# Attention head steps 8 to 11: probabilities and values as fp16 pairs, transposed by DMA, in place of fp32 on TensorE

## The chip, the cores and the metric

The kernel runs on one core of a Trainium2 chip. The metric is the device time of one execution in microseconds (us), as the median of several runs. Beside it there is one execution taken by the hardware profiler, from which all rows below come. TensorE is called PE here, VectorE DVE, ScalarE ACT, GpSimd POOL, and SP is the engine that only issues DMAs.

## The reference, cut to what matters

A decayed causal attention is followed by two feed-forward stages; only the attention and the first stage lie near the change.

```python
scores = q @ k.T / sqrt(D) + (cum[:, None] - cum[None, :])   # causal; cum = cumsum(log f)
attn = softmax(scores)                                       # B=4, H=8, S=576, D=64
x = (attn @ v) -> [B*S, H*D] = [2304, 512]
h = relu(x @ w_in); y = (h*h) @ w_out                        # d_ff = 2048
out = top-2 of 8 experts on y                                # 1024 wide each
```

## The kernel before, in words

**Attention is cut in two.** The first 256 positions of each batch (the head) are done early in twelve steps, numbered j = 0 to 11 (`subs`). Steps 8 to 11 are the second 128 queries of batches 2 and 3, four attention heads each. One head step is: fp32 scores S (`hd_s`, L397 to L408, on two PSUM banks of 512 columns), row maximum on DVE (`hd_max`, L419), exponentials on ACT (`hd_exp`, L430, result `pr`, fp32), eight fp32 transpositions of `pr` on PE (`hd_flip`, L436), their copy out of PSUM on ACT (`hd_copy`, L442, result `pth`), and eight fp32 products with V (`hd_pv`, L457), which the trace shows as sixteen records. After both steps of a batch the sum is normalized on DVE and ACT and turned into the columns of `xT` by a DMA (`att_turn`, L365). The positions from 256 on (the rest, units (b, i, p)) are done later; there P and V are already split into fp16 high and low parts (L277, L278, L208, L209), P is turned by a DMA (L279), and three fp16 products (L319) are made.

**The first feed-forward stage runs meanwhile.** It goes over chunks c of 384 tokens and over 16 weight tiles i: `mm1` (L554, twelve matmuls, one PSUM bank `m1`), relu and squares on ACT (L561, L562, L565), the low part g on DVE (L570), `mm2` (L616, nine matmuls). Passes: chunk 0 with weights 0 to 7 (in the hand-written order `PLAN`), chunk 1 with weights 0 to 7, then chunk 0 and chunk 1 with weights 8 to 15. Weights arrive packed and are unpacked by five operations each: three on DVE (L519, L524, L528), one on ACT (L531), and a last one on DVE (L534). They are staged in two buffers, so that the load of weight i+2, issued by POOL (L510), waits for the L534 of weight i. I write conv i for the five operations of weight i.

**What sets the order.** Up to the end of `PLAN` each engine's order is written out by hand; behind it a list scheduler with a cost model of its own places the instructions of all engines, once, ahead of the run. Each engine then goes through its row in order. `hd_tick(j)` at steps 8 to 13 of the feed-forward issues the head steps: the flip of step j-1, the scores of j, the PV of j-2.

**What is queued behind the weights.** POOL issues the last weight load (weight 15), then fills rows of the query sets (L178 to L180, 8.4 us), then issues the small DMAs `setk<-c` (L201), which bring the decay sums into the key sets. The scores of the rest (L226) wait for these. SP issues loads, spills and DMA transpositions in one row.

Of the kernel before, what the change touches and what calls it, by code (L numbers as in the profile page):

```python
# [7 lines left out]
F32 = mybir.dt.float32  # L8
F16 = mybir.dt.float16
# [31 lines left out]
NB = 2  # L41
# [18 lines left out]
R4 ch2 XT2 C31 ca3 E40 P3 cl2 h2 cb3 T40 lw4 E41 s3 l2 C40 T41 n3 cc3 S5 C41 ch3 XT3 R5 P4 h3 ca4 E50  # L60
m0 l3 cb4 E51 T50 cl3 r0 T51 cc4 lw5 X12 v21 C50 m1 g0 C51 ch4 S6 r1 cl4 g1 P5 R6 lw6 X13 v31 m2 s5 E60 ca5 a0 n5
r2 cb5 T60 h5 cc5 E61 m3 g2 ca6 ch5 l5 T61 r3 cb6 O5 a1 cl5 C60 C61 S7 g3 lw7 cc6 P6 R7 ch6 a2 cl6
E70 E71 m4 ca7 cb7 T70 r4 cc7 T71 C70 g4 a3 ch7 C71 cl7 m5 P7 r5 a4 s7 g5 n7 m6 h7 l7 O7 a5 r6
g6 m7 r7 g7
"""

# [2 lines left out]
def attn_moe_moe_kernel(ctx: ExitStack, tc, qka, qk, v, f, w_io, wgn, noise, w1, w2, out):  # L69
# [410 lines left out]
    def hd_xlow(j):  # L480
        b, i, a = subs[j]
        t0 = 128 * (B * i + b)
        nc.vector.tensor_tensor(xT[:, 1, :, t0:t0 + 128], hd["xf", j], xT[:, 0, :, t0:t0 + 128], op=ALU.subtract)  # L483

    def hd_tick(j, bank):
        if NPL <= j - 1 < NSUB:
            for z in range(2):
                hd_flip(j - 1, z, bank)
                hd_copy(j - 1, z)
        if j < NSUB:  # L490
            hd_s(j, bank)
            hd_max(j)
            for z in range(2):
                hd_exp(j, z)
        if NPL <= j - 2 < NSUB:
            hd_pv(j - 2)
            b, i, a = subs[j - 2]
            if a == i:
                att_sum(sums[b, i], 2, 2.0 ** -8, 1.6e-8)
                xs = att_norm(po_t[b, i], sums[b, i], 2)  # L500
                xh = att_high(xs, 2)
                att_low(xh, xs, 2)
                att_turn(b, i, xh)
# [482 lines left out]
    for tok in PLAN.split():  # L986
# [16 lines left out]
        elif tok[0] == "X" and tok[1] != "T":  # L1003
            hd_load(*d)
        elif tok[0] == "v":
            hd_load_v(*d)
        elif tok.startswith("lw"):
            pin["sp"] = load_w(d[0]).ins
        elif tok.startswith("c"):
            {"ca": conv_shift, "cb": conv_top, "cc": conv_rest, "ch": conv_high, "cl": conv_low}[tok[:2]](d[0])  # L1010
        elif tok[0] == "S":
            hd_s(d[0], start_bank if d[0] < NPX else main_bank)
        elif tok[0] == "R":
            hd_max(d[0])
        elif tok[0] == "E":
            hd_exp(*d)
        elif tok[0] == "T":
            hd_flip(d[0], d[1], flip_bank if d[0] < NPX else main_bank)
        elif tok[0] == "C":
            hd_copy(*d)  # L1020
        elif tok[0] == "P":
            hd_pv(d[0])
        elif tok[0] == "s":
            hd_sum(d[0])
        elif tok[0] == "n":
            hd_norm(d[0])
        elif tok.startswith("XT"):
            hd_xflip(d[0], xflip_bank)
        elif tok[0] == "h":
            if d[0] < NPX:  # L1030
                hd_xhigh(d[0])
            else:
                hd["xh", d[0]] = att_high(hd["n", d[0]], 2)
        elif tok[0] == "l":
            if d[0] < NPX:
                hd_xlow(d[0])
            else:
                att_low(hd["xh", d[0]], hd["n", d[0]], 2)
        elif tok[0] == "O":
            att_turn(subs[d[0]][0], subs[d[0]][1], hd["xh", d[0]])  # L1040
        elif tok[0] == "m":
            if psM is None:
                start_st.close()
                psM = mid_st.enter_context(tc.tile_pool(name="psM", bufs=1, space=PSUM))
            mm1_pe(0, d[0])
        elif tok[0] == "r":
            pin["act"] = mm1_act(0, d[0])
        elif tok[0] == "g":
            pin["dve"] = mm1_low(0, d[0])
        elif tok[0] == "a":  # L1050
            mm2(0, d[0])
        else:
            raise ValueError(tok)
# [223 lines left out]
```

## Time and profile before

| | |
|---|---|
| median of 3 runs | 985.39 us (984.55 to 988.39) |
| profiled execution: its own time | 986.78 us |
| its span, first to last instruction | 985.1 us |
| PE busy | 948.0 us (96%) |
| DVE busy | 563.3 us (57%) |
| ACT busy | 444.6 us (45%) |
| mean granted PE clock, 1 being full | 0.989 |

Busy time is the sum of an engine's instructions, overlaps counted once. Matmuls are pipelined, so a group's cost on PE is read from start to start and not from the duration of one. The head steps of the change lie between 88 and 141 us of the span.

### The profile page before, as it was taken

What the parts mean: (1) busy time and instruction counts of PE and PEld (TensorE: products, weight loads), DVE (VectorE), ACT (ScalarE), POOL (GpSimd) and SP (SyncE); (2) the same over time, 40 slices, a digit from 0 to 9 for tenths busy, and PEclk for the clock granted to TensorE, in tenths of its full rate; (3) what the DMA queues carried; (4) which work ended last, traced back from release to release, by engine and by line L of the source; (5) the groups of instructions that cost most, each with busy time, mean ns of one, the idle gap of its engine ahead of it and who ended that gap; (6) DMA issues with size and microseconds to landing.
All of it is one profiled execution on the core that took longest, in us unless ns stands there. A gap on an engine that the chain in (4) does not pass through costs nothing.

```text
span 985.1 us, 17576 instructions
## 1 busy us (share of the span) xinstructions
PE 948.0 (96%) x6866; PEld 552.9 (56%) x6866; DVE 563.3 (57%) x1240; ACT 444.6 (45%) x986; POOL 201.8 (20%) x238
## 2 busy tenths in 40 slices
PE   5899998999999999999999799999999999999996
PEld 3766664555555555555555344647475656565662
DVE  5884879777798778776477232436253434334221
ACT  3765659776577657645464120424141323223110
POOL 3000114004031021003002405244232314111202
PEclk9999999999999999999999899999999999999998
DMA  7374537695979949637295733698959494941303
GB/s 285 129 255 155 169 108 249 161 253 139 231 161 252 222 99 227 144 60 103 51 328 179 147 89 53 120 227 192 234 133 206 97 232 91 231 85 31 42 12 42
DMA packets 211255, 153.26 MB, mean 156 GB/s; under 512 B 166994, under 2 KB 177698, under 8 KB 209122
## 3 DMA queue, kind: packets, MB, share of 16 engines
q1 hardware_dynamic: 198994, 122.71, 49.5%
q0 software_dynamic: 12032, 29.35, 14.1%
q8 instruction: 55, 0.90, 0.4%
q14 instruction: 30, 0.25, 0.1%
q10 hardware_dynamic: 144, 0.05, 0.0%
HBM read 88.97 MB, written 23.98 MB: 115 GB/s over the span
## 4 chain that ended last, share of the span: by engine, by line
PE 76%; DMA 10%; issue 5%; DVE 4%; POOL 3%; ACT 1%; SPq 1%; ACTq 0%; POOLq 0%; DVEq 0%
PE e L882 18%; PE e L899 17%; PE m L554 15%; PE acc L616 14%; PE po L319 2%; DMA xgT<-xg 2%; DMA out_dram<-y,tix 2%; DMA wr<-in_w_dram 2%; DMA setk<-c 1%; PE psab L397 1%; PE po L457 1%; PE po L322 1%; DMA w<-in_w_io_dram 1%; PE ps L226 1%; PE ps L225 1%
## 5 line engine op out<-in xcount | busy, mean ns | idle before, releaser
L882 PE MATMUL e<-xgT,w1s 128*128 128x310 f16 (+2 forms) x1536 | 207.7, 297 | 6.0 <-DMA xgT<-xg 6.0
L899 PE MATMUL e<-w2s,hT 128*128 128x512 f16 (+1 forms) x960 | 209.3, 379 | 0.1
L616 PE MATMUL acc<-w,g 128*128 128x512 f16 x864 | 205.2, 379 | 0.4 <-DVE g L570 0.4
L882 PEld LDWEIGHTS <-w1s 128*128 128x128 f16 x1536 | 140.2, 98 | 72.4 <-issue 10.1
L886 ACT ACTIVATE hT<-e 128x310 f16<-128x310 f32 (+2 forms) x128 | 54.8, 429 | 269.4 <-PE e L882 269.1
L554 PE MATMUL m<-xT,w 128*128 128x384 f16 x960 | 173.1, 330 | 1.8 <-DVE xT L483 1.2
L899 PEld LDWEIGHTS <-hT 128*128 128x128 f16 (+1 forms) x960 | 99.5, 104 | 106.6 <-DVE hT L887 0.5
L554 PEld LDWEIGHTS <-w 128*128 128x128 f16 x1152 | 109.6, 99 | 77.1 <-issue 7.3
L616 PEld LDWEIGHTS <-g 128*128 128x128 f16 x864 | 81.5, 98 | 86.7 <-DVE g L570 0.7
L902 DVE TENSOR_SCALAR y<-e,gs 128x512 f32<-128x512 f32 (+1 forms) x40 | 30.0, 751 | 156.8 <-PE e L899 131.5
L887 DVE SCALAR_TENSOR_TENSOR hT<-e,hT 128x310 f16<-128x310 f32 (+2 forms) x128 | 60.8, 478 | 83.3 <-ACT hT L886 82.8
L903 POOL DMA_INDIRECT out_dram<-y,tix x40 | 65.6, 1641 | 164.2 <-DVE y L902 121.3
L764 POOL DMA_INDIRECT table<-ent,si x36 | 41.0, 1139 | 166.3 <-DVE si L761 156.8
L561 ACT ACTIVATE r<-m 128x384 f32<-128x384 f32 x80 | 39.1, 489 | 67.5 <-PE m L554 67.3
L254 DVE TENSOR_REDUCE sm<-ps 128x1 f32<-128x384 f32 (+2 forms) x96 | 53.3, 564 | 20.6 <-PE ps L242 9.4
L840 POOL DMA_INDIRECT xg<-x2d,tix x40 | 45.6, 1141 | 83.8 <-DMA xgT<-xg 53.5
L257 ACT ACTIVATE pr<-ps,sm 128x384 f32<-128x384 f32 (+1 forms) x64 | 40.1, 630 | 25.7 <-DVE sm L256 25.7
L562 ACT ACTIVATE g<-r 128x384 f16<-128x384 f32 x96 | 50.0, 521 | 1.8
L571 DVE TENSOR_TENSOR r<-r 128x384 f32<-128x384 f32 x64 | 35.5, 554 | 25.3 <-ACT g L562 25.1
L805 DVE SCALAR_TENSOR_TENSOR w2s<-wr,w2s 128x1024 f16<-128x1024 f32 x32 | 39.2, 1226 | 18.4 <-ACT w2s L804 18.4
L278 DVE TENSOR_TENSOR phl<-pr,phl 128x384 f16<-128x384 f32 (+1 forms) x64 | 38.6, 621 | 14.2 <-ACT phl L277 13.7
L805 DVE SCALAR_TENSOR_TENSOR w1s<-wr,w1s 128x1024 f16<-128x1024 f32 x32 | 38.9, 1224 | 11.9 <-ACT w1s L804 11.8
(276 smaller groups left out, 1076.4 us busy)
## 6 DMA issues: line engine op xcount, KB each, us to landing
wr<-in_w_dram SPq DMA_DIRECT2D x64, 512.0 KB, 4.7
qkr<-in_qk_dram SPq DMA_DIRECT2D x16, 896.0 KB, 5.8
w<-in_w_io_dram SPq DMA_DIRECT2D x8, 1024.0 KB, 4.8
w<-in_w_io_dram POOLq DMA_DIRECT2D x8, 1024.0 KB, 6.2
vr<-in_v_dram SPq DMA_DIRECT2D x16, 320.0 KB, 3.7
x2d<-x SPq DMA_DIRECT2D x18, 256.0 KB, 2.6
hraw<-in_qka_dram SPq DMA_DIRECT2D x8, 512.0 KB, 5.9
out_dram<-zero SPq DMA_DIRECT2D x5, 768.0 KB, 6.7
```

The source lines that it names most:

```text
L254: seen[u] = nc.vector.tensor_reduce(sm[:, z:z + 1], ps[z][:, :N], AX.X, ALU.max).ins
L554: nc.tensor.matmul(ps, W[i][:, wi, 0, 128 * cc:128 * cc + 128], xT[:, xi, cc, r0:r0 + CH], start=(x == 0), stop=(x == 11))
L562: nc.scalar.activation(g[:, 0, :], r, AF.Square, scale=2.0 ** -10)
L616: last[0] = nc.tensor.matmul(acc[t], g[:, gi, 128 * t:128 * t + 128], W[i][:, wi, 1, :], start=(i in ends[c][0] and x == 0), stop=(i in en ...
L764: s_ = nc.gpsimd.indirect_dma_start(out=table, out_offset=bass.IndirectOffsetOnAxis(ap=si[:, t, k:k + 1], axis=0), in_=ent[:, t, k, :], in ...
L805: nc.vector.scalar_tensor_tensor(lo, t_, sc, hi, op0=ALU.mult, op1=ALU.subtract)
L840: nc.gpsimd.indirect_dma_start(out=xg, out_offset=None, in_=x2d[0:seen, :], in_offset=bass.IndirectOffsetOnAxis(ap=rows_t[key, j][0], axis=0))
L882: last[0] = nc.tensor.matmul(ps[:, :hw], w1s[:, cc, wi, 128 * i:128 * i + 128], xgT[:, 4 * xi + cc, c], start=(x == 0), stop=(x == 11)).ins
L886: relu[0] = nc.scalar.activation(hi, ps[:, :hw], AF.Relu).ins
L887: nc.vector.scalar_tensor_tensor(hT[:, i, 1, c], ps[:, :hw], 0.0, hi, op0=ALU.max, op1=ALU.subtract)
L899: last[0] = nc.tensor.matmul(ps[:m], hT[:, i, hi, 128 * j:128 * j + m], w2s[:, i, wi, :], start=(i == 0 and x == 0), stop=(i == NFE - 1 an ...
L903: s_ = nc.gpsimd.indirect_dma_start(out=out, out_offset=bass.IndirectOffsetOnAxis(ap=ix[:m], axis=0), in_=y[:m], in_offset=None, compute_o ...
```

## The change

Steps 8 to 11 take the way of the later units. Values are split ahead of time (`hd_values`, tokens y0 to y3 in `PLAN`: one ACT and one DVE operation over 128x1024 each). P is split by two ACT and two DVE operations of 128x512 (`hd_split`), turned by one DMA transposition of 16 blocks on SP, and multiplied in 24 fp16 products of 64 columns (`hd_pv16`). Eight transpositions and eight fp32 products on PE and two copies on ACT go away in each step. The scale and floor of the sum follow the scale of V.

```diff
-E70 E71 m4 ca7 cb7 T70 r4 cc7 T71 C70 g4 a3 ch7 C71 cl7 m5 P7 r5 a4 s7 g5 n7 m6 h7 l7 O7 a5 r6
+E70 E71 m4 ca7 cb7 T70 r4 cc7 T71 C70 g4 y0 y1 a3 ch7 C71 cl7 m5 P7 r5 a4 s7 g5 y2 y3 n7 m6 h7 l7 O7 a5 r6
...
+    def hd_values(j):
+        b, i, a = subs[j]
+        vs = astream.tile([128, NB, 4, 2, 64], F16, name="vh", tag="vs", bufs=4)
+        vr = HV[b][:, :, 256 * a:256 * a + 256].rearrange("p k (h d) -> p k h d", h=4)
+        nc.scalar.activation(vs[:, :, :, 0, :], vr, AF.Copy, scale=64.0)
+        nc.vector.scalar_tensor_tensor(vs[:, :, :, 1, :], vr, 64.0, vs[:, :, :, 0, :], op0=ALU.mult, op1=ALU.subtract)
+        hd["v", j] = vs
+
+    def hd_split(j):
+        pr = hd.pop(("e", j))
+        phl = astream.tile([128, 4, 2, 2, 128], F16, name="phl", bufs=3)
+        pt = astream.tile([128, 4, 2, 2, 128], F16, name="pt", bufs=3)
+        for h in range(2):
+            pv = pr[:, h, :].rearrange("p (k s) -> p k s", s=128)
+            nc.scalar.activation(phl[:, :, h, 0, :], pv, AF.Copy)
+            nc.vector.tensor_tensor(phl[:, :, h, 1, :], pv, phl[:, :, h, 0, :], op=ALU.subtract)
+        nc.sync.dma_start_transpose(out=pt.rearrange("p a b c q -> p (a b c) q"), in_=phl.rearrange("p a b c s -> p (a b c s)"))
+        hd["t", j] = pt
+
+    def hd_pv16(j):
...
+        for p in range(2):
+            for z in range(2):
+                for kb in range(NB):
+                    for x, (vi, pi_) in enumerate(HL3):
+                        nc.tensor.matmul(po[:, a, z, p, :], pt[:, 2 * p + kb, z, pi_, :], vs[:, kb, 2 * p + z, vi, :],
+                                         start=(kb == 0 and x == 0), stop=(kb == i and x == 2), skip_group_check=True)
...
     def hd_tick(j, bank):
         if NPL <= j - 1 < NSUB:
-            for z in range(2):
-                hd_flip(j - 1, z, bank)
-                hd_copy(j - 1, z)
+            hd_split(j - 1)
...
-            hd_pv(j - 2)
+            hd_pv16(j - 2)
...
-                att_sum(sums[b, i], 2, 2.0 ** -8, 1.6e-8)
+                att_sum(sums[b, i], 2, 0.25, 1.024e-6)
...
+        elif tok[0] == "y":
+            hd_values(NPL + d[0] % NPL)
```

The scheduler places everything behind `PLAN` anew. In the changed file the lines behind the new functions stand 30 lower (L519 becomes L549, L534 becomes L564). SP's row of DMAs in the chunk-1 pass reads before (L365 turns x, L596 spills the accumulators, L643 to L665 set up the router's tables):

```order
29 L365 DMA_TRANSPOSE xT<-xh 128x8x128
30 L596 DMA part<-sp 128x1024 x3
31 L643 DMA wgr<-in_wgn_dram 128x64
32 L659 DMA table<-ini 128x8x8
33 L659 DMA table<-ini 128x8x2
34 L665 DMA table<-ino 128x8x28
35 L365 DMA_TRANSPOSE xT<-xh 128x8x128 x2
36 L596 DMA part<-sp 128x1024 x3
```

and now (L501 is the new transposition, L695 the old L665):

```order
29 L365 DMA_TRANSPOSE xT<-xh 128x8x128
30 L501 DMA_TRANSPOSE pt<-phl 128x16x128
31 L626 DMA part<-sp 128x1024 x3
32 L501 DMA_TRANSPOSE pt<-phl 128x16x128
33 L673 DMA wgr<-in_wgn_dram 128x64
34 L689 DMA table<-ini 128x8x8
35 L689 DMA table<-ini 128x8x2
36 L695 DMA table<-ino 128x8x28
37 L501 DMA_TRANSPOSE pt<-phl 128x16x128
38 L365 DMA_TRANSPOSE xT<-xh 128x8x128
39 L501 DMA_TRANSPOSE pt<-phl 128x16x128
40 L365 DMA_TRANSPOSE xT<-xh 128x8x128
```

The third transposition (step 10) stands right behind the table DMA, and the fourth behind the turn of batch 2.

DVE's row late in the chunk-1 pass, before (w_1384 is weight 11, w_1440 weight 12, L570 a g):

```order
131 L524 SCALAR_TENSOR_TENSOR w_1384<-w_1148,w_1384 128x1024
132 L528 SCALAR_TENSOR_TENSOR w_1148<-w_1148,w_1384 128x1024
133 L346 TENSOR_TENSOR xh<-xs,xh 128x512
134 L570 TENSOR_TENSOR g<-r,g 128x384
135 L519 TENSOR_SCALAR w_1440<-w_1244 128x1024
136 L534 SCALAR_TENSOR_TENSOR w_1384<-w_1148,w_1384 128x1024
137 L524 SCALAR_TENSOR_TENSOR w_1440<-w_1244,w_1440 128x1024
```

and now (w_1420 is weight 11, w_1492 weight 12, L600 a g, L500 the new low part of P for step 11):

```order
142 L554 SCALAR_TENSOR_TENSOR w_1420<-w_1154,w_1420 128x1024
143 L600 TENSOR_TENSOR g<-r,g 128x384
144 L144 SCALAR_TENSOR_TENSOR c_85<-c_85,pm,fch 96x320
145 L331 TENSOR_SCALAR sums<-sums 128x8
146 L558 SCALAR_TENSOR_TENSOR w_1154<-w_1154,w_1420 128x1024
147 L500 TENSOR_TENSOR phl<-pr,phl 128x4x128
148 L332 RECIPROCAL sums<-sums 128x8
149 L500 TENSOR_TENSOR phl<-pr,phl 128x4x128
150 L600 TENSOR_TENSOR g<-r,g 128x384
151 L549 TENSOR_SCALAR w_1492<-w_1260 128x1024
152 L564 SCALAR_TENSOR_TENSOR w_1420<-w_1154,w_1420 128x1024
153 L554 SCALAR_TENSOR_TENSOR w_1492<-w_1260,w_1492 128x1024
```

The split of P stands inside the unpacking of weight 11, which ends two splits later in the row.

On PE the first product with weight 15 (mm1 of chunk 0), which has to wait for conv 15, stood behind mm2 of weights 12 to 14 for two of the three token blocks (w_1845 is weight 15, w_1540 weight 14):

```order
1308 L616 MATMUL acc_1660<-w_1540,g 128x512
1309 L616 LDWEIGHTS g
1310 L616 MATMUL acc_1660<-w_1540,g 128x512
1311 L554 LDWEIGHTS w_1845
1312 L554 MATMUL m_1996<-xT,w_1845 128x384
```

and now it stands directly behind the scores of the third unit, ahead of all mm2 of weights 12 to 14 (w_1897 is weight 15):

```order
1402 L226 LDWEIGHTS setq_1721
1403 L226 MATMUL ps<-setk_1720,setq_1721 128x384
1404 L227 LDWEIGHTS identw
1405 L227 MATMUL ps<-maskw,identw 128x128
1406 L584 LDWEIGHTS w_1897
1407 L584 MATMUL m_2048<-xT,w_1897 128x384
```

So mm2 of weights 12 to 14 no longer lies between conv 15 and its first use.

## Rows read from the trace of the kernel before

**Rows 1.** Page, part 1: busy us (share of the span) x instructions.

```profile
PE 948.0 (96%) x6866; PEld 552.9 (56%) x6866; DVE 563.3 (57%) x1240; ACT 444.6 (45%) x986; POOL 201.8 (20%) x238
```

**Rows 2.** Stretches: us, busy us (instructions) by engine, granted clock, DMA share, GB/s.

```profile
80.00:84.00 4.00, 4.00 (x28) 2.87 (x28) 1.44 (x3) 2.08 (x4) 0.00 (x0) 1.00 0.71 264
89.20:145.90 56.70, 56.70 (x365) 37.19 (x365) 42.07 (x64) 34.25 (x80) 4.07 (x15) 1.00 0.41 119
145.90:175.10 29.20, 24.41 (x149) 12.87 (x148) 28.16 (x43) 24.90 (x49) 11.56 (x17) 0.99 0.77 245
175.10:200.00 24.90, 24.88 (x191) 13.77 (x191) 18.56 (x41) 17.28 (x41) 0.20 (x1) 0.94 0.70 145
```

**Rows 3.** The chain that ended last, 143 to 176 us: start, us, what.

```profile
144.63 1.24 DVE w L534
...
147.09 2.35 POOL setq L178 x4
...
155.49 0.63 POOL setk L201
...
158.53 3.48 DMA setk<-c
...
170.62 4.45 DMA setk<-c
```

**Rows 4.** PE in order of time: start, us, line, out<-in, count.

```profile
89.23 2.12 PE L554 MATMUL m<-xT,w 128*128 128x384 f16 x12
91.19 2.11 PE L616 MATMUL acc<-w,g 128*128 128x512 f16 x9
93.13 1.04 PE L436 MATMUL psab<-identf,pr 128*128 128x128 f32 x8
94.10 1.16 PE L397 MATMUL psab<-hraw 64*128 64x128 f32 x8
...
95.52 2.12 PE L554 MATMUL m<-xT,w 128*128 128x384 f16 x12
...
103.29 1.89 PE L457 MATMUL po<-hv,pth 128*128 128x64 f32 x16
105.03 0.81 PE L616 MATMUL acc<-w,g 128*128 128x512 f16 x3
```

**Rows 5.** The same view at 216 us: fp16 PV of a later unit.

```profile
216.35 0.86 PE L319 MATMUL po<-vs,pt 128*128 128x64 f16 x24
217.05 2.11 PE L554 MATMUL m<-xT,w 128*128 128x384 f16 x12
```

**Rows 6.** Groups by line and shape: busy us, mean ns of one; idle before, releaser.

```profile
L278 DVE TENSOR_TENSOR phl<-pr,phl 128x512 f16<-128x512 f32 x32 | 21.5, 688 | 8.3 <-ACT phl L277 7.9
L277 ACT ACTIVATE phl<-pr 128x512 f16<-128x512 f32 x32 | 19.5, 629 | 0.2
L534 DVE SCALAR_TENSOR_TENSOR w<-w,w 128x1024 f16<-128x1024 f32 x16 | 19.6, 1227 | 4.0 <-ACT w L531 4.0
L531 ACT ACTIVATE w<-w 128x1024 f16<-128x1024 f32 x16 | 18.2, 1135 | 8.1 <-DVE w L528 8.1
```

**Rows 7.** DMA issues on SP: count, KB each, median us to landing.

```profile
pt<-phl SPq DMA_TRANSPOSE x32, 4.6
...
table<-ino SPq DMA_DIRECT2D x1, 112.0 KB, 11.7
```

**Rows 8.** PE in order of time behind a wait at 173 us.

```profile
175.12 0.48 PE L226 MATMUL ps<-setk,setq 70*128 70x384 f16 x1 [2.01 <-DMA setk<-c]
...
175.50 3.34 PE L554 MATMUL m<-xT,w 128*128 128x384 f16 x12
```

**Rows 9.** DVE: its longest wait in 84 to 149 us (total, times, longest), then conv 15.

```profile
DVE g L570 <- ACT r L565: 13.5, 5, 4.1
...
181.53 1.23 DVE L534 SCALAR_TENSOR_TENSOR w<-w,w 128x1024 f16<-128x1024 f32 x1 [0.46 <-ACT w L531]
```

More of the change, by code (lines that the diff above doesn't have):

```diff
@@ L483, in hd_xlow @@
         nc.vector.tensor_tensor(xT[:, 1, :, t0:t0 + 128], hd["xf", j], xT[:, 0, :, t0:t0 + 128], op=ALU.subtract)
+    def hd_values(j):
[16 more added lines that the diff above has]
+    def hd_pv16(j):
+        b, i, a = subs[j]
+        pt, vs = hd.pop(("t", j)), hd.pop(("v", j))
+        if a == 0:
+            po_t[b, i] = psP.tile([128, 2, 2, 2, 64], F32, name="po", tag="po", bufs=1)
+        po = po_t[b, i]
+        for p in range(2):
[4 more added lines that the diff above has]
+                                         start=(kb == 0 and x == 0), stop=(kb == i and x == 2), skip_group_check=True)
     def hd_tick(j, bank):
         if NPL <= j - 1 < NSUB:
-            for z in range(2):
-                hd_flip(j - 1, z, bank)
-                hd_copy(j - 1, z)
+            hd_split(j - 1)
         if j < NSUB:
```

## The prediction

> **What bounds the kernel now.** I read the page first: PE is busy 96% of the span [rows 1]. Then the table of stretches around the change [rows 2]. From 89.2 to 145.9 us, where all four head steps lie, PE is busy for the whole 56.7 us at full clock and DVE for 42.1: here PE sets the time. From 145.9 to 175.1 it is the other way round: DVE is busy 28.2 of 29.2 us, PE only 24.4. The reader is to see that the two stretches have different limits and that the change works in the first one. The chain of waits tells what holds the second [rows 3]: DVE ends the unpacking of weight 13 (144.63 to 145.87), POOL issues the last weight load behind it, fills the query rows (147.09 to 155.49), issues the small key DMAs, and PE waits for the second and the fourth of them, which land at 162.0 and 175.1. So PE's time saved ahead of 145 is worth something behind 175 only if conv 13 and the preparation of the key sets on DVE come earlier too.
>
> **What goes away on PE.** Prices are read from start to start. Eight transpositions of one step go from 93.13 to 94.10, 0.97 us; the sixteen records of one fp32 PV from 103.29 to 105.03, 1.74 us [rows 4]. Four steps, which look alike: 4 x (0.97 + 1.74) = 10.8 us.
>
> One rule of the Trainium skill gives another size here. The row shows eight transpositions in 0.97 us, 121 ns each, in a stretch with full granted clock [rows 2, 4]. The Trainium skill (TensorE: Matmul & The Clock Gate, Part 4: PE-mode transpose) gives about 275 ns for one transposition in a kernel; by that figure the 32 would be 8.8 us and the saving some 5 us larger. The starts follow each other at 121 ns, so the measured row decides.
>
> **What comes in on PE.** 24 fp16 products of 128x64 stand in the trace of before, in a later unit: from 216.35 to 217.05, 0.70 us [rows 5]. Four steps: 2.8 us. Net on PE: 10.8 - 2.8 = 8.0 us saved.
>
> **What comes in elsewhere.** DVE: two subtractions of 128x512 per step at 688 ns, eight in all, 5.5 us inside the first stretch; four of 128x1024 for V at 1227 ns, 4.9 us, at 77 to 85 us [rows 6]. The latter hide: from 80 to 84 DVE is busy 1.44 of 4 us [rows 2], and weight 7, which the hand-written row now unpacks some 2.4 us later (two of them stand ahead of it), is first used at 89.23 [rows 4]. Without this cover they would cost these 2.4 us once. ACT: eight splits at 629 ns take the place of eight copies of the same size out of PSUM, nothing; four of 128x1024 for V at 1135 ns, 4.5 us [rows 6], lie under the same cover. SP and the DMA engines: four transpositions of 16 blocks, landing about 4.6 us behind the issue [rows 7], in a stretch where DMA is busy 41% [rows 2]; bounds are zero if they land before PE asks, and PE's whole wait if not (below).
>
> **Where the saving goes.** I follow the new rows by hand with these durations. In the first stretch DVE then has 42.1 + 5.5 = 47.6 us of work and PE 56.7 - 8.0 = 48.7. They are level, where before PE had 14.6 us more. DVE's slack was mostly waiting for the squares of a step that PE had not reached (13.5 us [rows 9]); it now shrinks to almost nothing. Three places follow.
>
> First, the third PV. Ahead of it PE has, from 89.2, seven mm1 and six mm2 of 1.95 us, six halves of S of 1.42 (94.10 to 95.52) [rows 4] and two PV of 0.70, 35.3 us: it asks at about 124.4. P for it is split on DVE at about 117 (from 95, where step 8 is split, some 21 us of work stand in the row, and one of waits). The transposition stands on SP behind the table DMA of 112 KB, which waits for a small operation of DVE at about 115 and took 11.7 us to land before [rows 7]. If the transposition lands 4.6 us behind its issue, at 121.6, nothing waits; if it has to follow the table's DMA, which then lands near 126.7, it lands a little behind that and PE waits about 3 us. I take 3. The Trainium skill (DMA: Bandwidth & Descriptors, Queues, rings and completion order) says that a DMA engine takes the descriptors of one ring in ring order, and both DMAs are in SP's row. By that rule the wait is the 3 us; no run yet shows what follows a table DMA.
>
> Second, conv 13. With that wait PE ends the mm1 of step 6 at about 124.4 + 3 + 0.7 + two of 1.95 = 132. Its g can't start on DVE before ACT's three operations, near 133.7. Behind that g stand in DVE's row two operations of conv 12, all four of conv 13, one g and the normalizing of batch 3: 0.6 + 2 x 1.2 + 0.7 + 3 x 1.2 + 0.6 + 2 x 0.7 = 9.3, and three waits for ACT's parts and the fourth PV of about a microsecond each: 146, where it was before (145.87). So POOL's fill and the first key DMA stay. PE has run ahead by some 5 us, and its new row has more mm1 and mm2 (weights 11 to 14) ahead of the scores, so its waits for the first three key sets shrink; the fourth set, which landed at 175.1, comes at about 169, since weight 14 is then unpacked ahead of the key preparation.
>
> Third, weight 15. From 132 to its first product PE has eight mm1, seven mm2, the fourth PV and three pairs of scores, 32 us, and some 5 us of waits for the spill, the keys and the bank: 169. Conv 15 ends, behind 146, after conv 14, four key preparations of 3 us, the spill and eight small maxima and splits, some 27 us: 173 (before 182.8 [rows 9]). PE waits 4 us there. Behind a wait PE may also run at the lower of its two clocks: after 2.01 us of waiting one mm1 took 3.34 us [rows 8] in place of 2.12 [rows 4].
>
> The sum: 8.0 saved; 3 given back at the third PV; about 2 given back as PE trades its old waits (29.2 less 24.4 busy is 4.8 [rows 2]) for the wait for weight 15 and a clock dip. Left: 3.0. From 175 to 200 PE was full [rows 2], and I take what lies behind as fixed. The profiled execution took 986.78 us (span 985.1), the median is 1.4 lower; 986.8 - 3.0 = 983.8, or **982.4 us** as a median.
>
> **The rivals.**
>
> *All of it arrives.* No wait at the third PV, DVE keeps up, the key chain moves with PE: 985.4 - 8.0 = 977.4. For it: PE is the limit of the first stretch without a gap. Against it: DVE and PE are level there afterwards, and the chain behind 145.9 has POOL and DMA in it, which the change does not shorten.
>
> *Nothing of it arrives.* The chain from conv 13 to the fourth key set sets the time at 175, whatever PE did before, and the saved time turns up as waits on keys and weights: 985.4, within 1.5. For it: PE already waits 4.8 us there, and DVE is full [rows 2]. Against it: PE's row was made anew and has other work ahead of those waits.
>
> *Slower, by the third transposition.* If it lands after about 130, PE stands for 6 us or more at the third PV, the next mm1 is late by as much, DVE's conv 12 and 13 stand in the row behind the g of that step, and conv 13 ends near 150.4 in place of 145.9 (a wait of 6.5 in place of 3, and one microsecond of lower clock, in the sum above). The whole chain of POOL, keys and weight 15 moves by 4.5 us, 985.4 + 4.5 = 989.9 at most, as PE's other savings can't come in. It decides from a wait of about 5 us on. For it: SP's place behind the table DMA. Against it: most transpositions landed within 4.6 us.
>
> *The change does not do what it says* is no rival here: PE's rows do lose the transpositions, and the fp16 PV has a price in the trace.
>
> **How the numbers follow.** Part of it arrives: 0.48, at 982.4 (979 to 985). All of it: 0.20. Nothing: 0.21. Slower: 0.11. About 0.5%, 4.9 us, is what a measurement of this kernel can tell from no change; the line for faster is 980.5. All of the second case and a third of the first lie beyond it: 0.20 + 0.16 = 0.36. Slower by more than 0.5% (990.3) takes the worse half of the last case and other mishaps of a new schedule: 0.10. The rest, 0.54, is the same. The range goes from the whole saving, 977.4, to most of the loss, 988.5.
>
> **What would show it.** In the new profile: no L436 or L457 behind 90 us; four groups of 24 products of about 0.70 us each; DVE close to full from 90 to 145; a wait of PE on the transposed P at the third PV (right if 2 to 4 us; if none, the first rival gains; if above 5, the loss); the end of conv 13 near 146; a wait at the first product with weight 15; the fourth key set some 5 us earlier. The forecast is wrong if DVE has slack from 90 to 145 and PE never waits there, or if the part of the row behind 200 us changes by more than 2 us, which I took as fixed.

## The result and the profile after

The changed kernel takes 992.21 us (median of 8 runs, 988.61 to 996.66), the kernel before 986.60 beside it (8 runs, 981.97 to 990.46): ratio 1.0063, interval 1.0036 to 1.0090. It is slower by some 6 us, where 982.4 was forecast, and lies above the range, which ended at 988.5. A second measurement of the same file gave 1.0056 (1.0030 to 1.0083). The profiled execution shown here is the slowest of the eight, 996.66 us; 3.4 us of its surplus are there at the first matmul of the expert layer (564.87 us, before 561.51), the rest arose in the expert layers and did not come again in the second profile.

Page of the changed kernel, part 1 (answers to [rows 1]):

```profile
PE 945.9 (95%) x6866; PEld 545.1 (55%) x6866; DVE 568.1 (57%) x1252; ACT 446.1 (45%) x990; POOL 202.8 (20%) x238
```

Stretches of the changed kernel, with the columns of [rows 2]; the last three are details of the second and third:

```profile
89.20:145.90 56.70, 54.23 (x389) 30.87 (x388) 46.93 (x75) 37.23 (x87) 4.80 (x15) 1.00 0.70 161
145.90:175.10 29.20, 20.62 (x105) 10.54 (x104) 23.90 (x33) 19.60 (x35) 17.79 (x17) 0.88 0.62 207
175.10:200.00 24.90, 22.11 (x165) 11.75 (x165) 17.20 (x40) 17.93 (x47) 0.00 (x0) 0.86 0.73 150
158.00:164.50 6.50, 0.02 (x1) 0.10 (x1) 1.91 (x2) 5.65 (x9) 6.39 (x11) 0.73 0.42 149
164.50:168.00 3.50, 3.42 (x12) 1.58 (x12) 2.79 (x5) 0.49 (x1) 0.00 (x0) 0.53 0.23 36
180.00:184.00 4.00, 4.00 (x23) 2.22 (x22) 1.50 (x3) 3.42 (x10) 0.00 (x0) 0.50 0.44 143
```

PE stands for 2.5, 8.6 and 2.8 us in the three stretches, 13.8 in all, against 4.8 in [rows 2]. The granted clock falls from 0.99 to 0.88 and from 0.94 to 0.86; over 29.2 and 24.9 us that is 3.2 and 2.0 us more. Of these, 1.8 us (0.27 of the 6.5 us from 158.0 to 164.5) fall where PE stands anyway and count once. 9.0 + 5.2 - 1.8 lost, 8.0 saved: 4.4 us slower by this account. In the trace the last product of mm2 starts at 559.3 us, before at 555.1, so 4.2 us later; the medians lie 5.6 apart. From 158.0 to 164.5 PE does nothing at all, and behind that it gets 0.53, near the lower of its two levels (1.2 of 2.4 GHz). What it waits for, longest first (in all, times, longest; 88 to 205 us):

```profile
PE ps L226 <- DMA setk<-c: 6.6, 1, 6.6
PE m L584 <- ACT r L591: 1.6, 3, 0.6
PE m L584 <- ACT w L561: 1.3, 1, 1.3
PE po L514 <- DVE c L143: 0.9, 1, 0.9
```

The first row is the loss: the scores wait for the key DMA. In the kernel before, over the same stretch, these waits were shorter:

```profile
PE ps L226 <- DMA setk<-c: 3.1, 3, 2.0
```

On PE of the changed kernel, in order of time:

```profile
117.21 0.87 PE L514 MATMUL po<-vh,pt 128*128 128x64 f16 x24
117.92 2.12 PE L584 MATMUL m<-xT,w 128*128 128x384 f16 x12
119.87 2.75 PE L646 MATMUL acc<-w,g 128*128 128x512 f16 x12
...
125.46 0.87 PE L514 MATMUL po<-vh,pt 128*128 128x64 f16 x24 [0.88 <-DVE c L143]
...
164.58 0.48 PE L226 MATMUL ps<-setk,setq 70*128 70x384 f16 x1 [6.56 <-DMA setk<-c]
...
165.86 3.69 PE L646 MATMUL acc<-w,g 128*128 128x512 f16 x12
```

Twelve products of mm2 take 3.69 us behind the wait; at full clock they took 2.75 (at 119.87). Why the key DMA is late stands in POOL's row:

```profile
147.05 0.53 POOL L540 DMA_DIRECT2D w<-in_w_io_dram  x1 [7.51 <-DVE w L564]
147.62 2.34 POOL L178 MEMSET setq<- 6x640 f16 x4
150.03 8.65 POOL L179 TENSOR_SCALAR_AFFINE_SELECT setq<-setq 6x320 f16<-6x320 f16 x1
158.64 0.45 POOL L180 TENSOR_SCALAR_AFFINE_SELECT setq<-setq 6x320 f16<-6x320 f16 x1
...
162.62 1.77 POOL L201 DMA_DIRECT2D setk<-c  x3
```

The load of weight 15 is issued at 147.05, 0.9 us behind the 146.15 of before, as forecast. The fill then takes 15.0 us (147.62 to 162.62) instead of 8.4 [rows 3]. One select of 6x320, which otherwise takes 0.45 us, takes 8.65. It depends on nothing but POOL's own memset. What DVE does in that time (its rows, in order, with no gap up to 158.36):

```profile
148.87 1.22 DVE L558 SCALAR_TENSOR_TENSOR w<-w,w 128x1024 int32<-128x1024 int32 x1
150.02 1.40 DVE L198 SCALAR_TENSOR_TENSOR setk<-setk,half,qkr 128x1152 f16<-128x1152 f16 x1
151.34 0.81 DVE L199 TENSOR_TENSOR setq<-qkr,setq 64x640 f16<-64x640 f32 x1
152.08 0.81 DVE L209 SCALAR_TENSOR_TENSOR vs<-vr,vs 128x640 f16<-128x640 f32 x1
...
157.69 0.67 DVE L549 TENSOR_SCALAR w<-w 128x1024 int32<-128x1024 int32 x1
159.98 1.55 DVE L198 SCALAR_TENSOR_TENSOR setk<-setk,half,qkr 128x1152 f16<-128x1152 f16 x1 [1.62 <-ACT setk L196]
```

In between lie the preparation of a second key set, the end of weight 14 (L564) and two g. Apart from the L549, which has one input, every operation reads two tensors from the on-chip memory; the select does not end in it either but 0.3 us after it, when DVE pauses. In the kernel before, the same selects met other neighbours. POOL first, then DVE:

```profile
150.60 0.45 POOL L179 TENSOR_SCALAR_AFFINE_SELECT setq<-setq 6x320 f16<-6x320 f16 x1
...
151.83 1.42 POOL L180 TENSOR_SCALAR_AFFINE_SELECT setq<-setq 6x320 f16<-6x320 f16 x1
153.22 0.76 POOL L179 TENSOR_SCALAR_AFFINE_SELECT setq<-setq 6x320 f16<-6x320 f16 x1
153.94 1.56 POOL L180 TENSOR_SCALAR_AFFINE_SELECT setq<-setq 6x320 f16<-6x320 f16 x1
```

```profile
149.83 1.88 DVE L595 SCALAR_TENSOR_TENSOR sp<-acc,sp 128x512 f16<-128x512 f32 x3
151.63 1.31 DVE L534 SCALAR_TENSOR_TENSOR w<-w,w 128x1024 f16<-128x1024 f32 x1
152.87 0.80 DVE L570 TENSOR_TENSOR g<-r,g 128x384 f16<-128x384 f32 x1
153.71 1.48 DVE L198 SCALAR_TENSOR_TENSOR setk<-setk,half,qkr 128x1152 f16<-128x1152 f16 x1
155.11 1.06 DVE L199 TENSOR_TENSOR setq<-qkr,setq 64x640 f16<-64x640 f32 x1
```

Beside L595, whose one input comes out of PSUM, a select takes 0.45 us; beside L534, with two inputs from the on-chip memory, 1.42. So the select seems to wait for a DVE operation with two such inputs, and in the changed kernel some ten of these follow each other. That alone does not make it long: the next two selects of the kernel before, beside a g and an L198, took 0.76 and 1.56 us. Each got through at the border between two such operations, and DVE's L199 behind took 1.06 us where it takes 0.81 in the changed kernel. In the changed kernel the one select got through at none of the borders. What decides between the two, the rows do not show.

### The profile page after: what moved, and what is told of

Same layout as the page of the kernel before. It is cut to its first block, busy times and chain, and to the rows that moved or that the text cites. A ratio compares the mean times of both kernels' runs of the same rounds, so it can differ in the third digit from the quotient of the medians.

```text
span 995.0 us, 17613 instructions
## 1 busy us (share of the span) xinstructions
PE 945.9 (95%) x6866; PEld 545.1 (55%) x6866; DVE 568.1 (57%) x1252; ACT 446.1 (45%) x990; POOL 202.8 (20%) x238
## 4 chain that ended last, share of the span: by engine, by line
PE 68%; issue 13%; DMA 10%; DVE 4%; POOL 3%; ACT 1%; SPq 0%; POOLq 0%; DVEq 0%
PE e L912 18%; PE e L929 17%; PE m L584 12%; PE acc L646 11%; DMA pt<-ph 2%; PE po L319 2%; DMA out_dram<-y,tix 2%; DMA xgT<-xg 2%; PE ps L226 1%; PE ps L225 1%; PE psab L397 1%; POOL out_dram L933 1%; PE po L322 1%; DMA xg<-x2d,tix 1%; DMA hv<-in_v_dram 1%
## 5 line engine op out<-in xcount | busy, mean ns | idle before, releaser
L929 PE MATMUL e<-w2s,hT 128*128 128x512 f16 (+1 forms) x960 | 212.5, 383 | 3.3 <-ACT hT L916 2.9
L794 POOL DMA_INDIRECT table<-ent,si x36 | 37.8, 1051 | 156.7 <-DVE si L791 146.9
L870 POOL DMA_INDIRECT xg<-x2d,tix x40 | 43.3, 1081 | 88.2 <-DMA xgT<-xg 55.3
L835 DVE SCALAR_TENSOR_TENSOR w1s<-wr,w1s 128x1024 f16<-128x1024 f32 x32 | 38.9, 1224 | 13.9 <-ACT w1s L834 13.8
```

The costliest lines, as they stand in the source:

```text
L835: nc.vector.scalar_tensor_tensor(lo, t_, sc, hi, op0=ALU.mult, op1=ALU.subtract)
L870: nc.gpsimd.indirect_dma_start(out=xg, out_offset=None, in_=x2d[0:seen, :], in_offset=bass.IndirectOffsetOnAxis(ap=rows_t[key, j][0], axis=0))
L929: last[0] = nc.tensor.matmul(ps[:m], hT[:, i, hi, 128 * j:128 * j + m], w2s[:, i, wi, :], start=(i == 0 and x == 0), stop=(i == NFE - 1 an ...
```

## The experiments

**Theories.** A, the stall: POOL's fill is slowed by what DVE runs beside it, and this delays the keys and PE. Its rivals: the loss is DVE's (the splits of P push the unpacking and the key preparations back, and POOL's late keys cost little); it comes from the splits and transpositions themselves; or, W, from the chain of weight loads, which the changed row disturbs. Ratios are to the kernel before on the same chip, with 95% intervals.

**The change again.** `same_again` is the changed file, not edited.

> The changed kernel once more, without an edit. Theory A (POOL is held by DVE): POOL's selects on the query rows read on-chip memory and stand still while DVE runs operations with two on-chip inputs one behind the other; DVE's row is fixed, so one select is again several us long (8.7 us in the first profile), the first key DMA lands near 164 again and PE waits 5 to 7 us for it; 0.4 to 0.9% slower than before. Theory B (the new order of PE's row costs the time, POOL's long select was chance): the long select is gone or short, the time is as slow all the same. Both expect that the 2.9 us wait at 704 us in the expert layers, seen once, need not come back.

Measured 1.0056 (990.08 us). The stall is there again, in POOL's row and in PE's wait for the keys, 6.6 us:

```profile
147.81 8.64 POOL L179 TENSOR_SCALAR_AFFINE_SELECT setq<-setq 6x320 f16<-6x320 f16 x1
```

The execution shown is the fastest of its eleven, 983.09 us, and faster than the profiled one of the kernel before (986.78). So the stall is read from the rows, and its price only from medians.

**The fill taken away.** `fill_early`: POOL fills set 0 at about 80 us, ACT copies it to the other three.

```diff
-        with tc.issue_after(pin["pool"]):
-            nc.gpsimd.memset(q2, -8.0)
-            nc.gpsimd.affine_select(q2[:, 0], ...)
-            nc.gpsimd.affine_select(q2[:, 1], ...)
+        if n:
+            nc.scalar.activation(QQ[n][64:70, 1], QQ[0][64:70, 1], AF.Copy)
...
+        elif tok == "q0":
+            fill_first()
```

> The changed kernel, but the query rows of the first key set are filled by POOL at about 80 us, where it is idle, and ACT copies them to the other three sets. Theory A: the first key DMA is issued behind the first key preparation of DVE (about 151.5) and lands by 155; PE's wait of 6.6 us there goes down to under 1.5 us, and with it the stretch of lower clock behind it; 5 to 8 us faster than the changed kernel, 984 to 988. Theory B: the wait goes elsewhere (weight 15, the bank), under 2 us gained, 990 to 993.

Measured 0.9984 (0.9955 to 1.0014): the loss is gone. The key DMAs go out at 150.73, 153.42, 160.06 and 164.50, and PE's wait for them is 2.2 us (under 1.5 expected). With this edit the scheduler also makes new rows: PE's, DVE's and ACT's differ from those of the changed kernel from 148 us on.

**Is it the reading?** Two kernels like `fill_early`, with sixteen dummy operations of POOL on a tile of their own at the place of the fill: sixteen writes, or eight writes and eight selects, which read as well.

```diff
+  if w_i + 2 == NF - 1:
+      for x in range(16):
+          with tc.issue_after(pin["pool"]):
+              pin["pool"] = (nc.gpsimd.memset(dm[0], -8.0) if x < 8 else nc.gpsimd.affine_select(dm[0], dm[0], ...)).ins
```

> The same as with the early fill, with 16 writes of a constant (6 x 160, a scratch tile) added on POOL between the last weight load and the key DMAs, where the fill stood; they read nothing. Theory A: they run through in some 2 to 4 us, though DVE is as busy as before, and the time is that of the early fill within 1.5 us. Theory B: the same.

> As the run with 16 writes, but 8 of the 16 are selects on the scratch tile, which read and write it; every other instruction of all engines in the same order. Theory A: at least one select lasts several us, as long as DVE's run of operations with two on-chip inputs (150 to 158 us), and the first key DMA lands near 160 or later; 3 to 7 us slower than with the 16 writes. Theory B: selects of this size take 0.3 to 0.5 us each, within 1.5 us of the run with writes.

POOL's row with writes, then with reads:

```profile
146.71 4.45 POOL L1172 MEMSET dm<- 6x160 f16 x16
151.64 0.62 POOL L211 DMA_DIRECT2D setk<-c  x1 [0.48 <-DVE setq L208]
```

```profile
145.64 2.20 POOL L1172 MEMSET dm<- 6x160 f16 x8
147.92 10.14 POOL L1172 TENSOR_SCALAR_AFFINE_SELECT dm<-dm 6x160 f16<-6x160 f16 x8
158.02 2.45 POOL L211 DMA_DIRECT2D setk<-c  x3
```

Eight small writes take 2.2 us, eight small selects 10.1, on data that nobody waits for. PE then waits longer for the keys, first with writes, then with reads:

```profile
PE ps L236 <- DMA setk<-c: 1.7, 1, 1.7
```

```profile
PE ps L236 <- DMA setk<-c: 6.4, 1, 6.4
```

In time it is 1.0026 (1.0002 to 1.0050) against 1.0003 (0.9983 to 1.0023): 2.2 us where 3 to 7 were expected, and the intervals overlap. PE, DVE and ACT go through the same order in both kernels, so this is the cleanest pair. That reads are held up and writes are not is shown; a price in time clear of noise this pair does not show.

**The same edit on the kernel before.** `before_fill_early` makes the edit of `fill_early` there.

> The kernel before (fp32 transpositions and products kept) with the same early fill. Theory A (the stall of POOL under DVE's run is what the change brought): before, the fill ended at 155.5 and the second key DMA, which waits for DVE's key preparation at 158.5 anyway, was the one PE waited for; so little is gained, 0 to 1.5 us, 984 to 986, and the changed kernel with the early fill is 1 to 3 us faster than this. Theory C (the fill is a cost of its own in both kernels, and the change is worth nothing): the kernel before gains as much as the changed one did, 5 to 7 us, about 979.5.

Measured 1.0063 (1.0038 to 1.0087), a miss. In that row the three copies on ACT, 0.73 us each, stand between the key preparations, and the key DMAs go out at 156.68, 159.77, 166.59 and 175.37. The edit was not neutral, so the fill was moved in another way, on POOL alone: sets 0 and 1 at about 80 us, sets 2 and 3 behind the load of weight 14. In the kernel before, every other engine keeps its order.

```diff
-... E71 m4 ca7 ...
+... E71 m4 q0 q1 ca7 ...
...
+                if w_i + 2 == NF - 2:
+                    for n_ in (2, 3):
+                        fill(n_)
```

> The kernel before with POOL's fill moved and nothing else: sets 0 and 1 at about 80 us, sets 2 and 3 behind the load of weight 14; every other engine keeps its order row for row, and no copy is added on ACT. Theory A: the first key DMA (issued at 155.5 before) can't go ahead of DVE's first key preparation, which ended at 155.2, and the second waited for DVE in any case; 0 to 1 us gained, 984.5 to 986. Theory C (the fill costs both kernels alike): 5 to 7 us gained. It also tells whether the loss of 5 us in the other early fill of the kernel before came from the three copies on ACT (then it is gone here) or from the fill's place.

> The changed kernel with the same move of POOL's fill and no copies on ACT (behind 146 us its rows come out in another order than with the copies). Theory A: no select is long, the first key DMA is issued near 151, the fourth near 164 or earlier; 982 to 986, and 1 to 3 us faster than the kernel before with the same move. Theory D' (the gain of the first early fill was the luck of its order): 988 or more.

Measured: before with the move 0.9991 (0.9971 to 1.0011), changed with the move 0.9987 (0.9960 to 1.0013). The move is worth some 7 us in the changed kernel (1.0056 to 0.9987) and nothing in the one before, as A has it. But in the changed kernel the rows behind the fill come out new as well, PE's from 154 us on and DVE's from 157, so the 7 us are not the price of the stall alone. It is also the second finding: in this pair, without the stall, the change itself brings nothing that can be measured.

**Parts of the change.** With the fill early: `half_batch3` changes steps 10 and 11 only, `half_batch2` steps 8 and 9. `additions_alone` is the kernel before with all splits and transpositions added and not read; PE keeps its old work. `no_low_part` is `fill_early` without the low part of P: one split, half the transposition, two products.

```diff
-            hd_split(j - 1)
+            if subs[j - 1][0] == 3:      # == 2 in half_batch2
+                hd_split(j - 1)
+            else:
+                for z in range(2):
+                    hd_flip(j - 1, z, bank)
+                    hd_copy(j - 1, z)
```

> With the early fill, and only steps 10 and 11 (batch 3) by fp16 and DMA; steps 8 and 9 go the old way. PE saves 4 in place of 8 us, DVE has half of the splits. Theory A (behind 146 us DVE's row and the keys set the time, PE's savings arrive only in part): within 1.5 us of the run with all four steps and early fill. Theory D (PE's saved time arrives once POOL is free): 3 to 4 us slower than all four steps.

> With the early fill, and only steps 8 and 9 (batch 2) by fp16 and DMA. No transposition stands behind the table DMA, and no split inside the unpacking of weights 11 and 12. Theory A: the end of weight 13's unpacking comes 1 to 3 us earlier than with all four steps, and the time is within 2 us of it, rather faster. Theory D: 3 to 4 us slower than with all four steps, as PE saves 4 us less.

> The kernel before with all that the change adds outside of PE (four splits of V, eight of P on ACT and on DVE, four transpositions on SP), their results unread; fp32 transpositions and products stay, and the old late fill too. Theory A: 10.4 us more of DVE work and 4 transpositions delay the unpacking of weights 11 to 13 by 1 to 4 us, and all that hangs on it; 1 to 4 us slower than before, without the long select unless DVE's key preparation comes to stand right at the fill. Theory D: DVE has 14.6 us of slack in that stretch; within 1 us of before.

> With the early fill by copies, and the low part of P left out in the four steps: no subtraction on DVE (8 x 688 ns), transpositions of 8 in place of 16 blocks, 16 in place of 24 products. This leaves out the low part's share of the output. Theory E (DVE's row sets when weights 11 to 13 and the key sets are ready, and the fourth key set sets the rest): weight 13 ends 3 to 5 us earlier than with all parts, the fourth key DMA is issued by about 161, and the time is 2 to 4 us shorter than with all parts, 979.5 to 982. Theory D (PE's work sets it): only PE's 0.9 us less, 982.5 to 984.

Measured 1.0038 (1.0007 to 1.0068), 1.0010 (0.9979 to 1.0042), 1.0101 (1.0071 to 1.0131) and 1.0066 (1.0045 to 1.0088). No half brings a gain over the kernel before. Against `fill_early` (0.9984) they are slower by 0.54% and 0.26%, 5 and 3 us; theory A expected 1.5 and 2 at most, its rival D 3 to 4, as PE saves 4 us less. Nor did the load of weight 15 come earlier in `half_batch2` (145.74; 145.60 in `fill_early`). So this speaks for D: some of PE's saving does seem to arrive there, though each half has new rows of its own. The additions cost 10 us where 1 to 4 were expected, and without a long select (the fill went from 145.68 to 154.02): DVE prepared the keys later, and the key DMAs went out at 157.79, 160.58, 167.48 and 178.33, before at 155.49, 158.53 and, the fourth, 170.62 [rows 3]. PE's longest wait there is for DVE's preparation:

```profile
PE ps L225 <- DVE setk L198: 3.5, 1, 3.5
```

`no_low_part` missed on the other side: less work, more time. The scheduler made another row, in which the load of weight 11 was issued at 116.64 us instead of 113.67 and DVE stood 3.63 us for it:

```profile
125.76 0.69 DVE L554 TENSOR_SCALAR w<-w 128x1024 int32<-128x1024 int32 x1 [3.63 <-DMA w<-in_w_io_dram]
```

So an edit that lets the scheduler make a new row can shift the time by several us on its own; a single one proves little here, and pairs with the same edit on both kernels were used from here on.

**The router's tables.** Their DMAs stand ahead of the third transposition. `tables_early` brings them at about 86 us and leaves the fill; `both_moves` and `before_both_moves` move tables and fill.

```diff
-        if (n, i) == (1, 1):
-            with tc.issue_after(pin["sp"]), tc.issue_after(pin["pool"]):
-                router_setup()
...
+        elif tok == "rs":
+            router_setup()
```

> The changed kernel with the tables brought forward alone; POOL's fill stays where it was. Theory W with A: DVE's key preparations come earlier by some 3 us, and POOL's fill, which needs the load of weight 15 issued before it, too; the long select stays (6 to 9 us), PE's wait for the first key set stays at 4 to 7 us; 987 to 990, 1 to 3 us better than the changed kernel. Theory K: 989.5 to 992.

> The changed kernel with POOL's fill moved (no copies on ACT) and, besides, the set-up of the router's tables (three table DMAs, with their POOL and DVE operations) brought forward to about 86 us, where the DMA engines are nearly idle (share 0.02 to 0.3 from 84 to 96 us). Theory W (behind the freed key chain, the chain of weights through two staging buffers holds the rest: load 11, its unpacking, load 13, its unpacking, load 15; and the table DMAs delay load 11): load 11 lands within 6 us of its issue, the third transposition lands sooner, the load of weight 15 is issued at 142 to 144 in place of 146.1, and the time falls by 2 to 4 us against the moved fill alone, to 980.5 to 983. Theory K (the key preparations and ACT and DVE behind 146 us hold the rest, whatever the weights do): within 1 us of the moved fill alone.

> The kernel before with the same two moves; PE, DVE, ACT and SP keep nearly the order of before. Theory W: PE has no gap before 146 us there, so weights that land sooner are worth nothing or little, 984 to 986, and the changed kernel with both moves is 2 to 5 us faster than this: the change's own worth once two obstacles are gone. Theory K: 984 to 986 too, and the changed kernel within 1.5 us of it.

Measured 1.0061 (1.0038 to 1.0085), 0.9965 (0.9938 to 0.9993) and 1.0008 (0.9982 to 1.0033). With the tables away and the fill in place, the stall and the loss stay (1 to 3 us of gain were expected). Three selects get through, each behind one DVE operation with two inputs, and the fourth is caught:

```profile
148.54 0.97 POOL L179 TENSOR_SCALAR_AFFINE_SELECT setq<-setq 6x320 f16<-6x320 f16 x1
149.48 1.56 POOL L180 TENSOR_SCALAR_AFFINE_SELECT setq<-setq 6x320 f16<-6x320 f16 x1
151.00 1.02 POOL L179 TENSOR_SCALAR_AFFINE_SELECT setq<-setq 6x320 f16<-6x320 f16 x1
151.99 8.56 POOL L180 TENSOR_SCALAR_AFFINE_SELECT setq<-setq 6x320 f16<-6x320 f16 x1
```

With both moved the change is 0.43% ahead of its control, 4 us, the best pair for it in which the control lost nothing by the edit. The load of weight 15 went out at 145.56 with the tables moved, at 147.05 and 144.83 in the two traces of the changed kernel: the chain of weights gained nothing that is clear, and W explains little.

**Keys early.** Key and value sets 0 and 1 are prepared two feed-forward steps earlier, on top of the moved fill.

```diff
+        if n == 1 and i in (5, 7):
+            p_ = (5, 7).index(i)
+            with tc.issue_after(pin["dve"]), tc.issue_after(pin["act"]):
+                prep(0, p_)
+                prep_v(0, p_)
+            load_qk(0, p_ + 2)
+            load_v(0, p_ + 2)
```

> The changed kernel with POOL's fill moved (no copies) and the key and value preparations of sets 0 and 1 placed two and no feed-forward steps earlier, so that they go into DVE's gaps ahead of 146 us; sets 2 and 3 follow in their place. Theory K (the key preparations behind 146 us hold what PE saved): the first two key DMAs go out by 146, the fourth by 161, PE's waits between 146 and 180 fall from 8 to under 4 us; 979.5 to 982.5, 2 to 5 us faster than with the moved fill alone. Theory W (weights): the preparations stand ahead of weight 13's unpacking, weight 15 comes later by as much as the keys come sooner; 984 to 987.

> The kernel before with the moved fill and the same earlier key preparations. Up to 146 us PE has no gap there, and only its 4.8 us of waits behind can shrink. Theory K: 983 to 986, and the changed kernel with the same edits 2 to 5 us faster than this. Theory W: 985 to 988, and no difference to the changed kernel beyond 1.5 us.

Measured: changed 0.9988 (0.9957 to 1.0019), before 0.9923 (0.9893 to 0.9954). The gain on the kernel before is real. In the changed one it failed for a reason that A names: the selects of set 3 now met the dense stretch of DVE.

```profile
145.98 14.87 POOL L183 TENSOR_SCALAR_AFFINE_SELECT setq<-setq 6x320 f16<-6x320 f16 x2
160.81 0.60 POOL L208 DMA_DIRECT2D setk<-c  x1
161.40 0.57 POOL L547 DMA_DIRECT2D w<-in_w_io_dram  x1
```

The key DMA and the load of weight 15 are queued behind two selects of 14.87 us, and PE waits 9.6 us for the keys. Of the two, one ended at 153.3, while DVE ran an L632 (one input from PSUM, 152.92 to 153.60), the other at 160.85, in a maximum over PSUM (160.46 to 161.00). An earlier maximum over PSUM (158.39 to 158.93) did not let it through.

Two more kernels: `all_moves` adds the tables' move to `keys_early`; `keys_early_free` has no late select at all (POOL fills sets 0 to 2 at about 80 us, ACT copies set 3).

> The changed kernel with all three moves: POOL's fill, the router's tables, and the key preparations of sets 0 and 1. Theory K: 978.5 to 982, the fastest of all. Theory W: no better than the fill and the tables moved, 982.5 to 985.

> As the run with early keys, which had a pair of POOL selects of 14.9 us (146.0 to 160.9) with the load of weight 15 and a key DMA queued behind it; here no select stands late: POOL fills sets 0 to 2 at about 80 us (the rows of set 2 are free there, since the changed kernel needs the identity no more), ACT copies set 3, and all other rows stay nearly as in that run. Theory A: no POOL operation above 2 us between 120 and 180 us, the third and fourth key DMA are issued by 151 and 160, the load of weight 15 by 146, PE's wait of 9.6 us is gone; 7 to 10 us faster than with the late selects, 978 to 981, and 0 to 4 us faster than the kernel before with early keys (981.2): what PE's 8 us are worth with all three obstacles gone. Rival (the keys' early place itself was what cost): 985 or more.

Measured 0.9932 (0.9905 to 0.9960), 979.69 us; and 0.9938 (0.9911 to 0.9965), 979.11 us. Without late selects the key DMAs go out at 131.39 to 156.93 and the 9.6 us are gone; by the ratios that is 0.50%, 5 us (7 to 10 expected). Both versions beat both kernels, but `before_keys_early`, without the change, is as good (0.9923, 981.21 us): the gain is that of the early keys.

**Where PE's 8 us go without the stall.** Stretch 145.9 to 175.1, early keys, without the change and with it (`keys_early_free`):

```profile
145.90:175.10 29.20, 28.30 (x176) 15.36 (x174) 29.18 (x52) 26.32 (x57) 2.62 (x4) 1.00 0.92 255
```

```profile
89.20:145.90 56.70, 54.88 (x398) 31.86 (x396) 50.58 (x80) 41.93 (x94) 6.34 (x17) 1.00 0.84 186
145.90:175.10 29.20, 24.26 (x145) 12.63 (x143) 25.66 (x44) 21.87 (x46) 2.29 (x3) 0.94 0.88 234
```

Without the change PE stands for 0.9 us there, and from 89.2 to 145.9 not at all. With it PE stands for 1.8 and 4.9 us, 5.9 more, and the clock of 0.94 costs 0.06 x 29.2 = 1.8: together 7.7 of the 8.0 saved. Its longest waits in the two stretches are for a transposed P of a later unit (2.7 us), for ACT's relu (1.7 in three) and for DVE's spill (1.5): no single engine. What the change is worth without the stall is read from three pairs: -0.04% (fill), -0.43% (fill and tables) and +0.15% (`keys_early_free` against `before_keys_early`, which moves the fill in another way), each uncertain by 0.3 to 0.4%. Two more pairs have the same edit but another disturbance on one side: -0.79% with the fill by copies, where the kernel before lost 6 us by the edit, and +0.65% with early keys, where the changed kernel has the stall.

## Why the prediction was wrong

**Right: what happens ahead of 146 us.** Conv 13 ended at 146.75 (146 predicted). The third PV was asked for at 124.58 (124.4 predicted). 24 products took 0.71 us from start to start (117.21 to 117.92; 0.70), so PE's saving of 8.0 stands. The 275 ns that the prediction took from the Trainium skill (TensorE: Matmul & The Clock Gate, Part 4: PE-mode transpose) are no contradiction to its 121: in the trace of before one fp32 transposition lasts 273 ns (median), and the next one starts 121 ns behind it. No fp32 transposition or PV is left behind 90 us. PE had to wait for the third transposition until 125.46, 1.5 us behind the landing of the table DMA at 123.94 (its own landing is not in the trace). That agrees with the order within a ring that the prediction took from the Trainium skill (DMA: Bandwidth & Descriptors, Queues, rings and completion order). But the wait was 0.9 us, not 3: the table landed 9.7 us behind its issue and not 11.7. That most transpositions land within 4.6 us was a misreading, as 4.6 is the median. DVE was busy for 46.93 us of the first stretch (47.6), which is not "close to full", and PE idled there for 2.5. Weight 15 cost a wait of 1.3 us at 178.5, not 4 at 169.

**The step that failed:** "So POOL's fill and the first key DMA stay". The end of conv 13 stayed within 0.9 us and the load behind it too, but the fill was taken for a fixed 8.4 us. Its length hangs on what DVE runs beside it, and on whether a select gets through between two operations there. In the kernel before, five of the eight selects got through while DVE worked mostly out of PSUM (L595), and three got through behind one operation each. In the changed kernel that work of DVE came ahead of the selects, and two key preparations and the end of weight 14 followed each other beside them; one select waited for all of it, the fill took 15.0 us, and the key DMAs came at 162.62 instead of 155.49. So "its waits for the first three key sets shrink" was turned round: one wait of 6.6 us, where before the waits for keys came to 3.1 in three. Nor did the fourth set come earlier: issued at 171.45, before at 170.62. This is shown from four sides: the move of the fill gives 7 us back in the changed kernel and nothing in the one before; dummy reads on POOL are stretched and dummy writes are not; moving the tables instead leaves stall and loss; and the early keys fail with late selects and succeed without. How much of the loss is the stall's alone is not shown: the two edits that give 7 us back bring new rows with them, and the one pair with equal rows, the probes, gives 2.2 us for 4.7 us more of waiting for keys.

What holds up a select is read from the rows: DVE operations with two inputs from the on-chip memory. The five long ones (8.65, 8.64, 8.56 and the pair of 14.87 us) ended when DVE paused or took an input out of PSUM, shorter ones between two such operations. No run took these operations of DVE away. The Trainium skill (SBUF — State Buffer, Who interferes with whom) states a rule for it: DVE's second input from the on-chip memory and GpSimd's reads go through one shared port, so a DVE operation with two such inputs holds up a GpSimd operation that reads there, and not one that only writes. The probes agree: 2.2 us for eight writes, 10.1 for eight reads. The rule was not weighed in the prediction; by it the fill has no fixed time.

**The size behind it:** "Left: 3.0" is not borne out even without the stall: three pairs put the change between 4 us faster and 1.5 slower, so it can't be told from nothing. The additions were priced at nothing outside PE, as DVE had room in the first stretch on average; put in alone they cost 10 us, in a row that the scheduler had made anew, so this is no clean price of theirs. The rival "nothing of it arrives" is what the kernel without the stall comes nearest to in two of the three pairs. The slower rival had the right consequence, the key chain late, but another place, the third transposition.

**Open:** what lets a select through between two DVE operations in one place and not in another, and which engine holds PE's row from 146 to 175 us once the keys are early. A kernel whose other engines keep the order of the change while only one gets faster was not built.

## What to carry to other kernels

Before a POOL operation that reads the on-chip memory is taken for a fixed time, look at DVE's row beside it: dense operations with two inputs from that memory can stretch it twentyfold, though they need not, and a DMA issue queued behind it on POOL is late by as much. Put such small fills where DVE is idle or reads PSUM. Where PE is relieved in a stretch that it bounds, the gain is worth no more than what the next stretch, bounded by others, lets through; test it with the same side edit on both kernels.

## What the runs showed of the hardware

- A select of POOL that waits beside DVE operations with two inputs from the on-chip memory can miss its turn at every border between them: 8.65, 8.64 and 8.56 us across some ten operations, 14.87 us for a pair. In other places it gets through behind one operation: three in a row in the kernel before (1.42, 0.76 and 1.56 us) and in `tables_early` (0.97, 1.56 and 1.02). Of eight small ones in `probe_reads`, the shortest took 0.31 us and the longest 4.72.
- The clock falls with the waits: 0.53 in the 3.5 us behind the wait of 6.6, 0.50 from 180 to 184 behind the wait for weight 15, 1.00 from 200 to 300, where PE was busy for 99.85 of 100 us.
- Executions of one kernel differ ahead of anything that was changed: over the first 89.2 us the granted clock was 0.92 in the profile of `both_moves`, 1.00 in that of `same_again`, 0.96 in that of the kernel before. So single profiles can't be compared to a few us, and ratios over many runs decide.
